# Conv-attention feeding an FFN: a new opening order, gated weight loads, throwaway matmuls and integer sums moved between engines

## Chip, cores and metric

One core of one Trainium2 chip runs the whole kernel. The metric is device time in microseconds (us), the median of the runs. TensorE (PE) multiplies matrices, VectorE (DVE), ScalarE (ACT) and GpSimd (POOL) do elementwise work, SyncE (SP) issues nearly all DMAs.

## Reference

```python
def _attn_ref(x, weight_gen):            # x (4, 4096, 192), weight_gen (4, 4096, 8, 7)
    w = softmax(weight_gen over the last axis)
    x_pad = six zero rows, then x
    out[b, s, h, g] = sum over k of w[b, s, h, k] * x_pad[b, s + k, h, g]   # 8 heads of 24 columns
    return out.reshape(B, S, D)

def _moe_ref(x, w_in, w_out):            # w_in (192, 2048), w_out (2048, 192), both float64 in memory
    h = x @ w_in
    return np.maximum(0.01 * h, h) @ w_out
```

Every token first gets a seven-tap convolution whose taps come out of a softmax, then goes through a two-layer network with a leaky ReLU.

## The kernel before

The 16,384 tokens lie 128 to a partition row. Each of 32 **chunks** takes four rows of every partition (512 tokens); two chunks make one **piece**, which is loaded (`load_weights`, `load_rows`) and put through the softmax together. The convolution of a chunk is seven multiplications and six additions of 768 columns (`conv_ops`); its result is transposed, multiplied by `w_in` (`mm1`), passed through the leaky ReLU (`leak`, `leak_out`) and multiplied by `w_out` (`mm2_...`). Each chunk has eight **steps** (`step(q)`), and a step is one `mm1` with two blocks of 128 hidden units and the `mm2` of earlier blocks.

From chunk 1 on every float32 operand is split into an upper and a lower half (F32R), and three products are summed. Chunk 0 multiplies in plain float32, because the halves of the weights aren't there yet. The weights arrive as float64 words, cut into 16 **keys** of 384 columns, eight of `w_in` and eight of `w_out`, in the order of the list `order`. Each is taken through stages: `read_words` (two ACT instructions, L114 and L115), `widen` (two DVE instructions, L123 and L126), an integer sum (`round_up` on POOL, L137, or L132 on DVE when `widen` is called with `add`), then `upper_half` (L155, ACT) and `lower_half` (L159, DVE), which only chunk 1 and later ones need. `read_words` also issues the load of a later key.

Chunk 0's convolution is shared: heads `0` to `G0` of its 32 row-head groups go to DVE, the others to POOL, and chunk 1's convolution is POOL's alone. The maximum, exponential and sum of the first piece are done in two halves of four rows, `FIRST` and `SECOND`. Later chunks come to TensorE not through its own transposes but by `split_h` (ACT, L307), `split_l` (POOL, L311), `squares` (DVE, L320) and `spread_squares` (L330), four groups of four DMAs from SP for each chunk.

The order in which all engines get their work, up to chunk 2, is written out by hand in the string `START`, one letter an item:

```python
    "ASrrgggggdddddagggggdddrwgggdddddobwTpp"   # start of the string before
```

`A`, `S` are the softmax of `FIRST`, `a`, `b` that of `SECOND`; `d` and `g` are one convolution operation of chunk 0 on DVE and POOL, `p` one of chunk 1 and `q` one of chunks 2 and 3 on POOL; `r`, `w`, `W`, `o`, `u`, `l` are the stages of the next key (`W` is `widen` with the sum on DVE; a capital `U` or `L` puts the half on DVE); `T` and `I` are the PE transposes of chunks 0 and 1 (L291), `k` and `K` the loads of the next piece, `M`, `E`, `D` its softmax, `C`, `V`, `y`, `Y`, `X` the way of chunk 2 to TensorE, and `s` is a step. Engines run their own items in this order and wait for each other by semaphores. `tell` puts a wait into SP's stream: what SP issues after it waits for the instruction told of.

The copies out of the transposes are at L296 and L298, chunk 0's second product at L438, those of later chunks at L399, the split of the hidden units at L373 and L374.

Of the kernel before, what the change touches and what calls it, by code (L numbers as in the profile page):

```python
# [8 lines left out]
F32 = mybir.dt.float32  # L9
F32R = mybir.dt.float32r  # L10
U32 = mybir.dt.uint32
AF = mybir.ActivationFunctionType
ALU = mybir.AluOpType
AX = mybir.AxisListType
PSUM = bass.MemoryType.PSUM

P = 128


HP = P // 2  # L20
# [3 lines left out]

C0 = 1

G0 = 24

NV = 12

START = (
    "ASrrgggggdddddagggggdddrwgggdddddobwTpp"
    "srwoppsrrWWoppKksrrWwoppsrrWwopMp"
    "suLrrWwoEppsuLrrWwoDpsuLuLrrWwoqqqsuLuLwoqqIs"
    "uLuLqqqsuLqqqsuLuLqqCVs"
    "uLuLsyYuLqqsuLXXqqsuLXXqqqsqqs"
)


# [1 line left out]
def conv_attention_moe_kernel(  # L41
# [8 lines left out]
    nc = tc.nc  # L50
    B, S, D = x.shape
    H, K = weight_gen.shape[2:]
    G = D // H
# [4 lines left out]
    PAD = K - 1  # L58
    J = 4
    TOK = J * P  # L60
# [3 lines left out]
    NB = D // HP  # L64
    BK = 32
    NK = P // BK
    HK = H * K
# [27 lines left out]
    def load_words(key, eng=nc.sync):  # L95
        q, kind = key
        if kind == IN:
            w = raw.tile([P, NB, P, 2], U32, tag="wi", name="wi_raw", bufs=3)
            for u, r in enumerate(HALVES):
                f = 2 * q + u  # L100
                eng.dma_start(out=w[r], in_=w_in_words[:, :, f * P:(f + 1) * P, :])
        else:
            w = raw.tile([P, 2, D, 2], U32, tag="wo", name="wo_raw")
            eng.dma_start(out=w, in_=w_out_words[:, 2 * q:2 * q + 2, :, :])
        words[key] = w
# [58 lines left out]
    R = 2 * J  # L164
# [6 lines left out]

    xt, wt, mx, sm = {}, {}, {}, {}

    def load_weights(q):
        r0 = piece[q] * R
        wt[q] = win.tile([P, R, HK], F32, tag="wt", name="wt")
        nc.sync.dma_start(out=wt[q], in_=w_rows[:, r0:r0 + R, :])

    def load_rows(q):
        r0 = piece[q] * R  # L180
        xt[q] = xin.tile([P, PAD + R, D], F32, tag="xt", name="xt")
        if r0 > 0:
            parts = ((0, PAD + R),)
            if q == 0:
                parts = ((PAD, PAD + J), (0, PAD), (PAD + J, PAD + R))
            for a, b in parts:
                nc.sync.dma_start(out=xt[q][:, a:b, :], in_=x_rows[:, r0 - PAD + a:r0 - PAD + b, :])
            return
        nc.sync.dma_start(out=xt[q][:, PAD:, :], in_=x_rows[:, 0:R, :])
        nc.gpsimd.memset(xt[q][0:1, 0:PAD, :], 0.0)  # L190
        for a, b in ((16, P), (1, 16)):
            nc.sync.dma_start(
                out=xt[q][a:b, 0:PAD, :], in_=x_rows[a - 1:b - 1, ROWS - PAD:ROWS, :]
            )
        for b in range(1, B):
            nc.gpsimd.memset(xt[q][b * PB:b * PB + 1, 0:PAD, :], 0.0)
# [3 lines left out]
    def grouped(q, s):  # L200
        return wt[q][:, s, :].rearrange("p r (h k) -> p (r h) k", k=K)
# [4 lines left out]
    def softmax_max(q, s=ALL):  # L206
        if q not in mx:
            mx[q] = win.tile([P, R * H, 1], F32, tag="mx", name="mx")
            sm[q] = win.tile([P, R * H, 1], F32, tag="sm", name="sm")
        m = mx[q][:, s.start * H:s.stop * H, :]  # L210
        nc.vector.tensor_reduce(out=m, in_=grouped(q, s), axis=AX.X, op=ALU.max)  # L211

    def softmax_sub(q, eng, s=ALL):
        eng.tensor_tensor(  # L214
# [12 lines left out]
    def softmax_div(q, eng, s=ALL, out=None):  # L227
        eng.tensor_tensor(  # L228
            out=grouped(q, s) if out is None else out, in0=grouped(q, s),
            in1=spread(sm[q], s), op=ALU.mult,  # L230
        )

    att, twice = {}, {}

    def conv_ops(c, eng, tag, g0=0, g1=J * H, tmp=None, w=None):

        if c not in att:
            att[c] = conv.tile([P, J, D], F32, tag="acc", name="acc", bufs=2)
        acc = att[c].rearrange("p r (h g) -> p (r h) g", g=G)[:, g0:g1, :]
        n = g1 - g0  # L240
        q, i0 = c // 2, c % 2 * J
        if w is None:
            w = wt[q].rearrange("p r (h k) -> p (r h) k", k=K)[:, i0 * H:(i0 + J) * H, :]
        for k in reversed(range(K)):
            xv = xt[q][:, i0 + k:i0 + k + J, :].rearrange("p r (h g) -> p (r h) g", g=G)
            wk = w[:, g0:g1, k:k + 1].to_broadcast([P, n, G])
            if k == K - 1:
                out = acc
            else:
                t = conv.tile([P, n * G], F32, tag=tag, name=tag) if tmp is None else tmp  # L250
                out = t[:, 0:n * G].rearrange("p (h g) -> p h g", g=G)
            eng.tensor_tensor(out=out, in0=xv[:, g0:g1, :], in1=wk, op=ALU.mult)  # L252
            yield
            if k < K - 1:
                if k > 0 or c > 1:
                    eng.tensor_tensor(out=acc, in0=acc, in1=out, op=ALU.add)  # L256
                    yield
                    continue
                if c not in twice:
                    twice[c] = xtp.tile([P, J * NB, 2, HP], F32, tag="sq", name="twice")  # L260
                sums = twice[c][:, g0 * G // HP:g1 * G // HP]
                for u in range(2 - c):
                    eng.tensor_tensor(  # L263
                        out=sums[:, :, u, :], op=ALU.add,
                        in0=att[c].rearrange("p r (b d) -> p (r b) d", d=HP)[:, g0 * G // HP:g1 * G // HP, :],
                        in1=t[:, 0:n * G].rearrange("p (b d) -> p b d", d=HP),
                    )
                yield

    def run(ops, n=None):  # L270
        while (n is None or n > 0) and next(ops, ops) is not ops:
            n = None if n is None else n - 1
# [138 lines left out]
    def tell(ins):  # L411

        told = nc.sync.nop().ins
        tc.add_manual_dep(told, ins.name, after, reason="rows to leave")
        return told
# [90 lines left out]
    with tc.manual_schedule():  # L506
        warm = const.tile([P, 1], F32, name="warm")
        nc.vector.memset(warm, 0.0)
        nc.scalar.activation(out=warm, in_=warm, func=AF.Exp)
        load_weights(0)  # L510
        load_rows(0)
        for key in order[0:4]:
            load_words(key)
        make_identity(nc, ident)
        sm_q = {}
        for q in range(2, NPIECE):
            sm_q[2 * q - 3] = q
# [81 lines left out]
        def spare():  # L599
# [3 lines left out]
            return spares[:, turn[0] % 2, 0:NW]  # L603

        w0 = po0[:, 0, 0:J * HK].rearrange("p (h k) -> p h k", k=K)
        conv0 = dict(
            d=conv_ops(0, nc.vector, None, 0, G0, spares.rearrange("p a b -> p (a b)"), w0),
            g=conv_ops(0, nc.gpsimd, "tmp0", G0, J * H),
            p=conv_ops(1, nc.gpsimd, "tmp"),
        )  # L610
        n, spreads = 0, 0
        for what in START.replace(" ", ""):
            if what in stages:
                prepare(what)
            elif what == "A":
                softmax_max(0, FIRST)
                softmax_sub(0, nc.vector, FIRST)
                softmax_exp(0, FIRST)
            elif what == "S":
                softmax_sum(0, FIRST)  # L620
                softmax_div(0, nc.vector, FIRST, w0[:, 0:J * H, :])
                softmax_div(0, nc.gpsimd, slice(J - C0, J))
            elif what == "a":
                softmax_max(0, SECOND)
                softmax_sub(0, nc.gpsimd, SECOND)
                softmax_exp(0, SECOND)
            elif what == "b":
                softmax_sum(0, SECOND)
                softmax_div(0, nc.gpsimd, SECOND)
            elif what in conv0:  # L630
                run(conv0[what], 1)
            elif what in "TI":
                transposes("TI".index(what))
            elif what == "K":
                load_weights(1)
            elif what == "k":
                load_rows(1)
            elif what == "M":
                softmax_max(1)
                softmax_sub(1, nc.gpsimd)  # L640
            elif what == "E":
                softmax_exp(1)
            elif what == "D":
                softmax_sum(1)
                softmax_div(1, nc.gpsimd)
            elif what == "q":
                feed(3, 1)
            elif what == "C":
                split_h(2)
            elif what == "V":  # L650
                split_l(2, nc.gpsimd)
            elif what in "yY":
                squares(2, "yY".index(what))
            elif what == "X":
                spread_squares(2, [spreads])
                spreads += 1
            elif what == "s":
                step(n)
                n += 1
            else:  # L660
                raise ValueError(what)
# [37 lines left out]
```

## Time and profile before

| | us |
|---|---|
| median of 3 runs | 1177.0 (1175.46 to 1177.43) |
| the profiled execution, its own time | 1179.21 |
| its span, first to last instruction | 1177.2 |
| PE busy | 1144.6 (97%) |
| POOL, ACT, DVE busy | 786.1, 645.7, 515.2 |
| mean granted clock of TensorE | 0.996 |

TensorE is busy nearly all the time, so the kernel can lose time in two ways only: TensorE waits, or it runs at its lower clock. Both happen nearly only in the first 120 us. The profiled execution stands 2.2 us above the median.

### The profile page before, as it was taken

To read this page: it belongs to the slowest core of one execution; us is meant where nothing else is said; L and a number is where in the kernel's file an instruction comes from. 1 tells how busy PE (TensorE), PEld (TensorE's weight loads), DVE (VectorE), ACT (ScalarE), POOL (GpSimd) and SP (SyncE) were. 2 spreads that over 40 slices of the span, in tenths; PEclk is the share of its full clock that TensorE was granted. 3 is DMA by queue.
4 is the path that set the end of the run, shared out by engine and by line. 5 is a ranking of instruction groups with operands and counts; after the bars stand their busy time and mean duration, and the time that the engine had idled before them with its cause. 6 is when DMAs were issued, how large, how long until landed. Compare 5 with 4: busy or idle time off the path is not lost.

```text
span 1177.2 us, 30212 instructions
## 1 busy us (share of the span) xinstructions
PE 1144.6 (97%) x12648; PEld 1072.1 (91%) x12648; DVE 515.2 (44%) x823; ACT 645.7 (55%) x1174; POOL 786.1 (67%) x499
## 2 busy tenths in 40 slices
PE   2998999999999999999999999999999999999998
PEld 1677999999999999999999999999999999999998
DVE  5674444434444434444443444434444433443432
ACT  2655555555555555556555555655555564555554
POOL 5787866678766668766668866667866667966300
PEclk9998999999999999999999999999999999999999
DMA  5612231323323142232323223142241324221220
GB/s 148 187 58 55 69 108 48 105 55 82 110 55 107 45 115 64 69 110 55 99 67 102 76 61 104 45 119 55 69 123 49 103 55 110 68 69 49 53 51 14
DMA packets 42950, 93.70 MB, mean 80 GB/s; under 512 B 9664, under 2 KB 25024, under 8 KB 41023
## 3 DMA queue, kind: packets, MB, share of 16 engines
q1 hardware_dynamic: 42670, 91.59, 28.6%
q8 instruction: 99, 1.62, 0.6%
q14 instruction: 37, 0.29, 0.1%
q10 hardware_dynamic: 144, 0.20, 0.0%
HBM read 31.98 MB, written 12.58 MB: 38 GB/s over the span
## 4 chain that ended last, share of the span: by engine, by line
PE 93%; DVE 2%; POOL 2%; DMA 1%; SPq 1%; issue 1%; ACT 1%; DVEq 0%; POOLq 0%; ACTq 0%
PE hp L351 46%; PE po L399 45%; PE po L438 2%; DMA xt<-in_x_dram 1%; SPq L330 1%; POOL acc L256 1%; POOL tmp L252 1%; DVE spares L252 0%; DVE wo L159 0%; DVE acc L256 0%; DVE gl L374 0%; ACT hp L357 0%; DVE wi_l L159 0%; DMA xx<-sq 0%; POOL bits L137 0%
## 5 line engine op out<-in xcount | busy, mean ns | idle before, releaser
L399 PE MATMUL po<-wo,gh 64*128 64x384 f32 x3968 | 632.2, 354 | 1.6 <-ACT gh L373 1.6
L399 PE MATMUL po<-wo,gl 64*128 64x192 f32 x3968 | 608.2, 248 | 0.7 <-DVE gl L374 0.7
L374 DVE TENSOR_TENSOR gl<-hp,gh 128x512 fp32r<-128x512 f32 x496 | 342.4, 691 | 554.9 <-ACT gh L373 554.9
L399 PEld LDWEIGHTS po<-wo,gh 64*128 64x128 f32 x3968 | 565.8, 185 | 8.1 <-ACT gh L373 1.8
L351 PE MATMUL hp<-xx,wi_h 64*128 64x512 f32 x2976 | 560.5, 397 | 3.7 <-DMA xx<-sq 2.4
L399 PEld LDWEIGHTS po<-wo,gl 64*128 64x128 f32 x3968 | 546.2, 188 | 1.7 <-DVE gl L374 1.5
L357 ACT ACTIVATE hp<-hp 128x512 f32<-128x512 f32 x496 | 292.5, 590 | 426.3 <-PE hp L351 399.3
L351 PE MATMUL hp<-xx,wi_l 64*128 64x512 f32 x1488 | 444.9, 393 | 0.0
L351 PEld LDWEIGHTS hp<-xx,wi_h 64*128 64x128 f32 x2976 | 407.9, 185 | 32.5 <-issue 2.4
L256 POOL TENSOR_TENSOR acc<-acc,tmp 128x768 f32<-128x768 f32 (+1 forms) x190 | 345.5, 1818 | 14.4
L373 ACT CAST gh<-hp 128x512 fp32r<-128x512 f32 x496 | 291.3, 587 | 43.9 <-PE po L399 30.1
L252 POOL TENSOR_TENSOR tmp<-xt,wt 128x768 f32<-128x768 f32 (+1 forms) x192 | 291.5, 1518 | 12.2
L351 PEld LDWEIGHTS hp<-xx,wi_l 64*128 64x128 f32 x1488 | 271.4, 185 | 19.9
L311 POOL TENSOR_TENSOR split<-acc,split 128x768 fp32r<-128x768 f32 x30 | 55.5, 1849 | 170.4 <-ACT split L307 170.4
L475 DVE TENSOR_TENSOR ot<-po,ot 128x384 f32<-128x384 f32 x62 | 34.5, 557 | 76.6 <-ACT ot L474 76.1
L214 POOL TENSOR_TENSOR wt<-wt,mx 128x448 f32<-128x448 f32 (+1 forms) x16 | 15.3, 953 | 72.5 <-DVE mx L211 72.4
L320 DVE STREAM_TRANSPOSE sq<-split 128x384 f32<-128x384 f32 x120 | 58.4, 543 | 0.0
L252 POOL TENSOR_TENSOR acc<-xt,wt 128x768 f32<-128x768 f32 (+1 forms) x32 | 48.5, 1516 | 0.2
L228 POOL TENSOR_TENSOR wt<-wt,sm 128x448 f32<-128x448 f32 (+2 forms) x17 | 15.7, 924 | 39.3 <-DVE sm L225 34.4
L474 ACT COPY ot<-po 128x384 f32<-128x384 f32 x62 | 29.7, 479 | 11.7 <-PE po L399 8.9
L307 ACT CAST split<-acc 128x768 fp32r<-128x768 f32 x30 | 25.1, 838 | 6.9 <-POOL acc L256 6.9
L291 PE MATMUL ta<-ident,twice 128*128 128x128 f32 x24 | 4.3, 351 | 21.6 <-DVE twice L263 21.6
(51 smaller groups left out, 235.9 us busy)
## 6 DMA issues: line engine op xcount, KB each, us to landing
xx<-sq SPq DMA_DIRECT2D x480, 96.0 KB, 2.1
xt<-in_x_dram SPq DMA_DIRECT2D x14, 1344.0 KB, 5.8
out_dram<-ot SPq DMA_DIRECT2D x63, 192.0 KB, 1.9
wt<-in_weight_gen_dram SPq DMA_DIRECT2D x16, 224.0 KB, 2.6
wi_raw<-in_moe_w_in_dram SPq DMA_DIRECT2D x16, 192.0 KB, 8.6
wo_raw<-in_moe_w_out_dram SPq DMA_DIRECT2D x8, 384.0 KB, 4.6
xt<-in_x_dram SPq DMA_DIRECT2D x2, 384.0 KB, 6.7
xt<-in_x_dram SPq DMA_DIRECT2D x1, 768.0 KB, 4.8
```

What stands on the lines that cost most here:

```text
L252: eng.tensor_tensor(out=out, in0=xv[:, g0:g1, :], in1=wk, op=ALU.mult)
L256: eng.tensor_tensor(out=acc, in0=acc, in1=out, op=ALU.add)
L307: nc.scalar.copy(out=split[c][:, 0], in_=att[c])
L311: eng.tensor_tensor(out=l, in0=att.pop(c), in1=h.bitcast(F32), op=ALU.subtract)
L320: nc.vector.transpose(out=sq[c][:, v, i], in_=src[:, v])
L351: nc.tensor.matmul(out=hp[2 * q + u], lhsT=w[s], rhs=r[s], start=(m == 0), stop=(m == len(passes) - 1),)
L357: return nc.scalar.activation(out=hp[n], in_=hp[n], func=AF.Prelu, alpha=0.01).ins
L373: nc.scalar.copy(out=h, in_=t)
L374: nc.vector.tensor_tensor(out=l, in0=t, in1=h.bitcast(F32), op=ALU.subtract)
L399: ins = nc.tensor.matmul(out=po[j // HALF][:, j % HALF, 0:d], lhsT=g[n][s, j * P:(j + 1) * P], rhs=wo[s, f, 0:d], start=(f == 0 and i < HA ...
L474: nc.scalar.copy(out=ot, in_=po[k][:, :, D:2 * D])
L475: nc.vector.tensor_tensor(out=ot, in0=po[k][:, :, 0:D], in1=ot, op=ALU.add)
```

## The change

Six edits, all of them in the opening:

1. The first load takes four rows of the softmax weights and two of the three parts of `x`; the other loads are issued behind a `tell` on the first maximum, and the second half of the softmax weights and the third part of `x` go between the words of `w_in`.
2. Chunk 0's convolution is cut at 20 of 32 groups rather than 24 for taps 6 to 1, and at 24 for tap 0.
3. Twelve products of zeros (`heat`) stand ahead of the transposes of chunk 0, behind the latest DVE operation of its convolution.
4. `W` stands in place of `w` and `o` for 14 of the 16 keys (7 before).
5. Two lower halves go to POOL (`l`), one upper half to DVE (`U`).
6. `START` is reordered: the convolution of chunk 1 is issued in one row, `k` comes ahead of `K`, and `X` stands behind steps 12 and 13 rather than 13 and 14.

```diff
-G0 = 24
+G0 = 20
 START = (
-    "ASrrgggggdddddagggggdddrwgggdddddobwTpp"
-    "srwoppsrrWWoppKksrrWwoppsrrWwopMp"
...
-    "uLuLsyYuLqqsuLXXqqsuLXXqqqsqqs"
+    "ASdrrggggdgddggdggadgdrwgZdgddddgdobTWrppppppppWpkKWrrspWrr..."
...
+    "YLusXqqqXqqsqqXqlXqsqs"
 )
...
-    def load_weights(q):
+    def load_weights(q, s=slice(0, R)):
...
-    def load_rows(q):
+    def load_rows(q, parts=((0, PAD + R),)):
...
-        nc.vector.tensor_reduce(out=m, in_=grouped(q, s), axis=AX.X, op=ALU.max)
+        return nc.vector.tensor_reduce(out=m, in_=grouped(q, s), axis=AX.X, op=ALU.max).ins
...
-    def conv_ops(c, eng, tag, g0=0, g1=J * H, tmp=None, w=None):
+    def conv_ops(c, eng, tag, inner=ALL_G, outer=ALL_G, tmp=None, w=None):
...
         for k in reversed(range(K)):
+            s = inner if k else outer
+            n = s.stop - s.start
...
+            if eng is nc.vector:
+                latest[c] = ins
...
-        load_weights(0)
-        load_rows(0)
-        for key in order[0:4]:
-            load_words(key)
+        load_weights(0, FIRST)
+        load_rows(0, ((PAD, PAD + J), (0, PAD)))
         make_identity(nc, ident)
+        zeros = const.tile([P, TOK], F32R, name="zeros")
+        nc.gpsimd.memset(zeros.bitcast(F32), 0.0)
...
-            d=conv_ops(0, nc.vector, None, 0, G0, spares.rearrange("p a b -> p (a b)"), w0),
-            g=conv_ops(0, nc.gpsimd, "tmp0", G0, J * H),
+            d=conv_ops(0, nc.vector, None, slice(0, G0), slice(0, (J - C0) * H), away, w0),
+            g=conv_ops(0, nc.gpsimd, "tmp", slice(G0, J * H), slice((J - C0) * H, J * H)),
...
+        def heat(n):
+            t = ps_h.tile([P, TOK], F32, tag="h", name="heat")
+            for m in range(n):
+                ins = nc.tensor.matmul(
+                    out=t, lhsT=zeros[:, 0:P], rhs=zeros, start=True, stop=True
+                ).ins
+                if m == 0:
+                    tc.add_manual_dep(ins, latest[0].name, after, reason="not before")
...
             elif what == "A":
-                softmax_max(0, FIRST)
+                tell(softmax_max(0, FIRST))
+                load_words(order[0])
+                load_weights(0, SECOND)
+                load_words(order[1])
+                load_rows(0, ((PAD + J, PAD + R),))
+                load_words(order[2])
+                load_words(order[3])
...
-                softmax_div(0, nc.gpsimd, slice(J - C0, J))
+                softmax_div(0, nc.gpsimd, slice(G0 // H, J))
...
+            elif what == "Z":
+                heat(12)
```

SP's first loads, before and now. `wt` are the softmax weights, `xt` rows of `x`, `wi_raw` and `wo_raw` words of `w_in` and `w_out`; the three `xt` of 768, 1152 and 768 columns are called the first, second and third part.

```order
L177 DMA wt<-in_weight_gen_dram 128x448
L187 DMA xt<-in_x_dram 128x768
L187 DMA xt<-in_x_dram 128x1152
L187 DMA xt<-in_x_dram 128x768
L101 DMA wi_raw<-in_moe_w_in_dram 64x3x256 x6
L104 DMA wo_raw<-in_moe_w_out_dram 128x2x384
```

```order
L176 DMA wt<-in_weight_gen_dram 128x224
L184 DMA xt<-in_x_dram 128x768
L184 DMA xt<-in_x_dram 128x1152
L99 DMA wi_raw<-in_moe_w_in_dram 64x3x256 x2
L176 DMA wt<-in_weight_gen_dram 128x224
L99 DMA wi_raw<-in_moe_w_in_dram 64x3x256 x2
L184 DMA xt<-in_x_dram 128x768
L99 DMA wi_raw<-in_moe_w_in_dram 64x3x256 x2
L102 DMA wo_raw<-in_moe_w_out_dram 128x2x384
```

The first `wt` is half as long, and SP's wait for the first maximum (not shown as a row) stands ahead of the first `wi_raw`.

POOL behind the convolution of chunk 0, before and now. `acc<-xt,wt` and `tmp<-xt,wt` are multiplications of chunk 1's convolution, `acc<-acc,tmp` its additions, `bits<-bits,rnd` the integer sums of keys.

```order
L228 TENSOR_TENSOR wt<-wt,sm 128x224
L252 TENSOR_TENSOR acc<-xt,wt 128x768
L252 TENSOR_TENSOR tmp<-xt,wt 128x768
L137 TENSOR_TENSOR bits<-bits,rnd 128x384
L256 TENSOR_TENSOR acc<-acc,tmp 128x768
L252 TENSOR_TENSOR tmp<-xt,wt 128x768
L137 TENSOR_TENSOR bits<-bits,rnd 128x384
L256 TENSOR_TENSOR acc<-acc,tmp 128x768
```

```order
L225 TENSOR_TENSOR wt<-wt,sm 128x224
L251 TENSOR_TENSOR acc<-xt,wt 128x768
L251 TENSOR_TENSOR tmp<-xt,wt 128x768
L256 TENSOR_TENSOR acc<-acc,tmp 128x768
L251 TENSOR_TENSOR tmp<-xt,wt 128x768
L256 TENSOR_TENSOR acc<-acc,tmp 128x768
```

Before, an integer sum stood between the operations of the convolution, and POOL waited there for DVE; now the convolution runs without one.

DVE behind the copy out of chunk 0's transposes (`xx<-ta`), before and now. `spares<-mag` and the row after it are `widen`, `bits<-spares,rnd` is the integer sum.

```order
L296 COPY xx<-ta 128x4x128
L123 TENSOR_SCALAR spares<-mag 128x384
L126 SCALAR_TENSOR_TENSOR bits<-mag,spares 128x384
L123 TENSOR_SCALAR spares<-mag 128x384
L126 SCALAR_TENSOR_TENSOR spares<-mag,spares 128x384
L132 ISA bits<-spares,rnd 128x768
```

```order
L295 COPY xx<-ta 128x4x128
L121 TENSOR_SCALAR spares<-mag 128x384
L124 SCALAR_TENSOR_TENSOR spares<-mag,spares 128x384
L130 ISA bits<-spares,rnd 128x768
L121 TENSOR_SCALAR spares<-mag 128x384
L124 SCALAR_TENSOR_TENSOR spares<-mag,spares 128x384
L130 ISA bits<-spares,rnd 128x768
```

Each key now has three DVE instructions here; nine keys in a row are made so, with one maximum between them.

## Rows read from the trace of the kernel before

**Rows 1.** Who PE waited for, from 0 to 140 us.
```profile
PE ta L291 <- DVE twice L263: 21.6, 1, 21.6
PE hp L351 <- DMA xx<-sq: 2.4, 2, 1.9
PE po L399 <- ACT gh L373: 1.6, 1, 1.6
PE hp L351 <- DVE xx L301: 1.4, 1, 1.4
PE hp L351 <- POOL bits L137: 0.6, 1, 0.6
PE po L399 <- DVE gl L374: 0.6, 2, 0.3
```
**Rows 2.** Windows of PE: stretch, its length, busy (instructions), granted clock, DMA share, GB/s.
```profile
95.08:98.50 3.42, 3.42 (x20) 0.50 0.02 5
112.16:119.00 6.84, 6.33 (x33) 0.50 0.08 19
...
119.00:1170.00 1051.00, 1050.84 (x11981) 1.00 0.28 76
```
**Rows 3.** Timeline of PE: start, duration, instruction, count, idle time before it.
```profile
21.65 2.79 PE L291 MATMUL ta<-ident,twice 128*128 128x128 f32 x12 [21.65 <-DVE twice L263]
24.37 6.62 PE L351 MATMUL hp<-xx,bits 64*128 64x512 f32 x24
31.58 2.85 PE L351 MATMUL hp<-xx,bits 64*128 64x512 f32 x12 [0.59 <-POOL bits L137]
34.36 2.87 PE L438 MATMUL po<-bits,g 128*128 128x192 f32 x16
```
**Rows 4.** Timeline of PE at the seam to chunk 1, and the window of one `mm1`.
```profile
65.01 1.53 PE L291 MATMUL ta<-ident,twice 128*128 128x128 f32 x12
...
76.01:78.21 2.20, 2.20 (x20) 1.00 0.31 110
```
**Rows 5.** DMA issues from 1.2 to 2.0 us: size and us to landing.
```profile
xt<-in_x_dram SPq DMA_DIRECT2D x1, 576.0 KB, 8.6
```
**Rows 6.** Windows of the DMAs: stretch, its length, granted clock, DMA share, GB/s.
```profile
2.00:5.50 3.50, 1.00 0.91 307
```
**Rows 7.** Timelines of DVE and POOL in chunk 0's convolution.
```profile
3.41 0.39 DVE L211 TENSOR_REDUCE mx<-wt 128x32 f32<-128x224 f32 x1 [2.54 <-DMA wt<-in_weight_gen_dram]
6.25 0.28 POOL L228 TENSOR_TENSOR wt<-wt,sm 128x56 f32<-128x56 f32 x1 [4.93 <-DVE po L228]
10.26 0.76 DVE L252 TENSOR_TENSOR spares<-xt,po 128x576 f32<-128x576 f32 x1 [3.37 <-DMA xt<-in_x_dram]
20.08 1.42 DVE L263 TENSOR_TENSOR twice<-acc,spares 128x576 f32<-128x576 f32 x2
```
**Rows 8.** Operations of POOL by form, from 0 to 92 us: busy, mean ns, idle before.
```profile
L256 POOL TENSOR_TENSOR acc<-acc,tmp 128x768 f32<-128x768 f32 x11 | 20.6, 1874 | 0.4
L252 POOL TENSOR_TENSOR tmp<-xt,wt 128x768 f32<-128x768 f32 x12 | 19.4, 1618 | 0.6
L137 POOL TENSOR_TENSOR bits<-bits,rnd 128x384 uint32<-128x384 uint32 x9 | 9.0, 999 | 9.0 <-DVE bits L126 9.0
L256 POOL TENSOR_TENSOR acc<-acc,tmp 128x192 f32<-128x192 f32 x5 | 2.9, 590 | 0.4
```
**Rows 9.** DVE from 22 to 67.58 us: the window, then its integer sums.
```profile
22.00:67.58 45.58, 30.31 (x50) 1.00 0.51 149
...
L132 DVE CUSTOM_DVE_ANT_0 bits<-spares,rnd 128x768 uint16<-128x768 uint16 x7 | 3.9, 557 | 0.3
```
**Rows 10.** Timeline of POOL: the last addition of chunk 2's convolution.
```profile
89.22 1.84 POOL L256 TENSOR_TENSOR acc<-acc,tmp 128x768 f32<-128x768 f32 x1
```
**Rows 11.** Timeline of SP, and the chain of waits: chunk 2's way to TensorE.
```profile
101.68 10.13 SPq L330 DMA_DIRECT2D xx<-sq  x16
...
111.22 2.12 DMA xx<-sq
```

More of the change, by code (lines that the diff above doesn't have):

```diff
@@ L25 @@
 C0 = 1
-G0 = 24
+G0 = 20
 NV = 12
 START = (
-    "ASrrgggggdddddagggggdddrwgggdddddobwTpp"
-    "srwoppsrrWWoppKksrrWwoppsrrWwopMp"
-    "suLrrWwoEppsuLrrWwoDpsuLuLrrWwoqqqsuLuLwoqqIs"
-    "uLuLqqqsuLqqqsuLuLqqCVs"
-    "uLuLsyYuLqqsuLXXqqsuLXXqqqsqqs"
+    "ASdrrggggdgddggdggadgdrwgZdgddddgdobTWrppppppppWpkKWrspWrrWsrrsWWMrpspWr"
+    "WruspLrUuWrLWuEsDrwrLsouWWuLLuqqWlqquqsqLLqquqqqIusLLusuqsLuLquCVyuqqLsL"
+    "YLusXqqqXqqsqqXqlXqsqs"
 )
@@ L172, in conv_attention_moe_kernel @@
     xt, wt, mx, sm = {}, {}, {}, {}
-    def load_weights(q):
+    def load_weights(q, s=slice(0, R)):
         r0 = piece[q] * R
-        wt[q] = win.tile([P, R, HK], F32, tag="wt", name="wt")
-        nc.sync.dma_start(out=wt[q], in_=w_rows[:, r0:r0 + R, :])
-    def load_rows(q):
+        if q not in wt:
+            wt[q] = win.tile([P, R, HK], F32, tag="wt", name="wt")
+        nc.sync.dma_start(out=wt[q][:, s, :], in_=w_rows[:, r0 + s.start:r0 + s.stop, :])
+    def load_rows(q, parts=((0, PAD + R),)):
         r0 = piece[q] * R
-        xt[q] = xin.tile([P, PAD + R, D], F32, tag="xt", name="xt")
+        if q not in xt:
+            xt[q] = xin.tile([P, PAD + R, D], F32, tag="xt", name="xt")
         if r0 > 0:
-            parts = ((0, PAD + R),)
-            if q == 0:
-                parts = ((PAD, PAD + J), (0, PAD), (PAD + J, PAD + R))
             for a, b in parts:
@@ L231, in softmax_div @@
         )
-    att, twice = {}, {}
-    def conv_ops(c, eng, tag, g0=0, g1=J * H, tmp=None, w=None):
+    att, twice, latest = {}, {}, {}
+    ALL_G = slice(0, J * H)
+    def conv_ops(c, eng, tag, inner=ALL_G, outer=ALL_G, tmp=None, w=None):
         if c not in att:
             att[c] = conv.tile([P, J, D], F32, tag="acc", name="acc", bufs=2)
-        acc = att[c].rearrange("p r (h g) -> p (r h) g", g=G)[:, g0:g1, :]
-        n = g1 - g0
+        acc = att[c].rearrange("p r (h g) -> p (r h) g", g=G)
         q, i0 = c // 2, c % 2 * J
@@ L244, in conv_ops @@
         for k in reversed(range(K)):
+            s = inner if k else outer
+            n = s.stop - s.start
             xv = xt[q][:, i0 + k:i0 + k + J, :].rearrange("p r (h g) -> p (r h) g", g=G)
-            wk = w[:, g0:g1, k:k + 1].to_broadcast([P, n, G])
+            wk = w[:, s, k:k + 1].to_broadcast([P, n, G])
             if k == K - 1:
-                out = acc
+                out = acc[:, s, :]
             else:
-                t = conv.tile([P, n * G], F32, tag=tag, name=tag) if tmp is None else tmp
+                t = conv.tile([P, J * D], F32, tag=tag, name=tag) if tmp is None else tmp
                 out = t[:, 0:n * G].rearrange("p (h g) -> p h g", g=G)
-            eng.tensor_tensor(out=out, in0=xv[:, g0:g1, :], in1=wk, op=ALU.mult)
+            ins = eng.tensor_tensor(out=out, in0=xv[:, s, :], in1=wk, op=ALU.mult).ins
+            if eng is nc.vector:
+                latest[c] = ins
             yield
[L254 to L267, printed above, removed]
-                yield
+            if k > 0 and k < K - 1 or k == 0 and c > 1:
+                eng.tensor_tensor(out=acc[:, s, :], in0=acc[:, s, :], in1=out, op=ALU.add)
+                yield
+        if c > 1:
+            return
+        if c not in twice:
+            twice[c] = xtp.tile([P, J * NB, 2, HP], F32, tag="sq", name="twice")
+        b = slice(outer.start * G // HP, outer.stop * G // HP)
+        av = att[c].rearrange("p r (b d) -> p (r b) d", d=HP)[:, b, :]
+        ov = t[:, 0:n * G].rearrange("p (b d) -> p b d", d=HP)
+        for u in range(2 - c):
+            eng.tensor_tensor(out=twice[c][:, b, u, :], in0=av, in1=ov, op=ALU.add)
+        yield
     def run(ops, n=None):
@@ L605, in conv_attention_moe_kernel @@
         w0 = po0[:, 0, 0:J * HK].rearrange("p (h k) -> p h k", k=K)
+        away = spares.rearrange("p a b -> p (a b)")
         conv0 = dict(
-            d=conv_ops(0, nc.vector, None, 0, G0, spares.rearrange("p a b -> p (a b)"), w0),
-            g=conv_ops(0, nc.gpsimd, "tmp0", G0, J * H),
+            d=conv_ops(0, nc.vector, None, slice(0, G0), slice(0, (J - C0) * H), away, w0),
+            g=conv_ops(0, nc.gpsimd, "tmp", slice(G0, J * H), slice((J - C0) * H, J * H)),
             p=conv_ops(1, nc.gpsimd, "tmp"),
         )
+        def heat(n):
[6 more added lines that the diff above has]
+                    tc.add_manual_dep(ins, latest[0].name, after, reason="not before")
         n, spreads = 0, 0
```

## Prediction, made before the changed kernel had run

> **What bounds the kernel now.** I read three views in this order. First, who PE waited for, from 0 to 140 us: 21.6 us for the first convolution, 0.6 for an integer sum on POOL, 1.4 for DVE's subtraction behind chunk 1's transposes, 1.6 and 0.6 for split hidden units, 2.4 for the DMAs that bring chunk 2 [rows 1]. Second, the windows: from 119 to 1170 us PE is busy 1050.84 of 1051.00 us at the full clock, so nothing can be gained there, while in two earlier stretches of 3.42 and 6.84 us the granted clock is 0.50 (1.2 of 2.4 GHz); both come behind waits of PE [rows 2]. Third, PE's own timeline: twelve transposes take 2.79 us at 21.65 but 1.53 in chunk 1, and the first 24 records of L351 take 6.62 us where twelve take 2.85 later [rows 3, 4]. The window view shows no lower level there, but these durations are those of the lower one. So the time is the start of the first transposes, plus PE's work, plus what is lost before 119 us. An edit counts only if it moves PE.
>
> **Part by part.**
>
> *Gated loads.* The second part of `x` lands 8.6 us after its issue [rows 5]; DVE waits 3.37 us for it, until 10.26 [rows 7]. Up to that part 224 + 384 + 576 = 1184 KB were issued; at 307 GB/s from 2.0 us they are through near 6.0 [rows 6], yet it landed at 10.2, with words moving beside it. Now 1072 KB go alone, through near 5.5 at the same rate. The bounds of the landing are thus 5.5 and 9.9 (10.24 less 112 KB at 307 GB/s). Anything up to 6.8 costs nothing, because DVE is in its first multiplication until then; I take that. What the wait on SP holds back are the words: they are issued behind the maximum, which ends at 3.80 [rows 7]; the first needed is widened behind DVE's fourth tap, at 11.3 by the next parts. So they may take some 6 us to land before the gate costs anything.
>
> The Trainium skill, page "DMA: Bandwidth & Descriptors", section "Queues, rings and completion order", says that each DMA engine consumes a queue's descriptors in ring order. By that rule what is issued behind the second part could not delay it, and the gate would bring only the 112 KB. The 4.2 us between 6.0 and 10.2 speak against it, though one late engine would look the same.
>
> *The convolution of chunk 0.* On DVE it lasted from 10.26 to 21.50 (the end of its last row) [rows 7], 11.24 us; ten of its operations shrink from 576 to 480 columns, by about 0.10 us each (0.76 us at 576, 0.39 for a reduction of 224), so 10.2 us remain: 6.8 + 10.2 = 17.0. POOL gets 288 columns instead of 192. An addition is 0.59 us at 192 and 1.87 at 768, so 0.80 at 288; a multiplication is 1.62 against 1.87, so 0.70 [rows 8]. With 0.08 between instructions five pairs are 8.3; the division (0.4, from 0.28 at 56), the first multiplication (0.7), the subtraction (0.6), tap 0 (0.6) and the doubled sum (1.1) make it 11.7 us from POOL's start at 6.25: 17.9. POOL ends last, and the transposes start at 17.9 instead of 21.65: **-3.8**. If the rows land at 9.9, DVE ends last at 20.1, and the term is -1.5.
>
> *Throwaway products.* They wait for DVE's fourth tap: 6.8 + four operations of 0.69 + the maximum 0.3 + two of 0.69 = 11.3. Eighteen products of half height, two side by side, take 2.2 us [rows 4], so one of 512 columns is 0.24 us at the full clock and 0.49 at the lower: twelve last 2.9 to 5.9 and end between 14.2 and 17.2. They hold up nothing; a gap of 0.7 to 3.7 us follows. If the clock is up when the transposes run, the gain is 2.79 - 1.53 = 1.3 there and 6.62 - 2 x 2.79 = 1.0 in the first products [rows 3, 4]: 2.3. If it isn't, 0. A loss is excluded, since PE ran there at the lower clock before. If it rises and falls again in the gap, one more stretch like that of 3.42 us [rows 2] takes 1.7 of the 2.3 back. I take the middle, **-1.2**, because both stretches at 0.50 came behind waits of about 2 us [rows 1], which is the middle of the gap.
>
> *Integer sums.* Seven of POOL's nine go; the nine were 9.0 us of work and 9.0 of waiting for DVE [rows 8]. PE's wait of 0.6 for one ends, since DVE makes the third key 5.3 us behind the transposes' start (the copy at 1.7, six instructions of 0.6) and PE wants it after 1.5 + 2 x 2.79 = 7.1: **-0.6**. DVE pays 7 x 0.56 = 3.9 us, a lower half more (about 1) and an upper half (0.6) on 30.3 us busy of 45.6 [rows 9], with some 3 us between its instructions: about 39. PE's chunk 0 is 1.5 + 14 x 2.79 = 40.5 us of work [rows 3], so DVE has 41. It fits, narrowly, if the words come in time. The 1.4 us at chunk 1's transposes came about because DVE still had a key to widen; I let 0.4 stand: **-1.0**, with bounds of -1.4 and +4.
>
> *The way to chunk 2.* POOL ended chunk 2's convolution at 91.06 [rows 10], and ACT, whose split of it stands ahead of two blocks of hidden units, kept PE waiting from about 91.5. With 16 us less of sums and waiting, some 1 us for a lower half taken over and up to 4 of waiting for the next piece's softmax, POOL ends between 75 and 80. PE is 6.6 us earlier by then and wants those blocks near 84.9. So the waits of 1.6 and 0.6 go, and with them the 3.42 us at half clock (1.7): **-3.9**. SP's sixteen DMAs were issued from 101.68 and landed 11.7 us later [rows 11], while PE had two steps of work from the products they are told of to chunk 2. A step is 4.4 us (239 of them in the 1051 us of [rows 2]): 8.8 us. The DMAs now stand one step earlier, so 13.2 us of work cover 11.7. The 2.4 us go, and with them 6.84 us at half clock with 6.33 busy (3.2): **-5.6**; as the margin is only 1.5 us, the other bound is 0.
>
> *The order of `k` and `K`, the upper half on DVE and the cut at 24 for tap 0* lie inside these sums.
>
> Sum: -3.8 - 1.2 - 0.6 - 1.0 - 3.9 - 5.6 = -16.1. Against the profiled execution's own 1179.2 that is 1163.1; it stands 2.2 above the median, so I forecast **1161** us.
>
> **Rivals.** (A) *The rows land no earlier* (ring order, as above, or a late engine): the first term is -1.5, the time 1163.3. For it: 8.6 us is long even for shared engines. (B) *The spread still ends last ahead of chunk 2*, because SP's DMAs need DVE's four transposes of squares, which stand behind more work: 1161 + 5.6 = 1166.6. (C) *DVE is late at chunk 1's transposes*: the wait of 1.4 stays or grows to 4, and a fall of the clock adds 1.7: up to 1167.7. (D) *Slower: DVE sets the pace of chunk 0.* PE wants a key every 2.79 us. A key costs DVE 1.8, and from the eighth on a lower half besides. Should a lower half cost over 1.0 on the mean beside POOL, PE waits in each product, its clock falls, and chunk 0's last ten products of 2.79 take 28 us more: 1161 + 28 = 1189. Against it: 39 us of work in 41. (E) *The savings don't reach PE*: what is gained ahead is waited for at a later chain that doesn't move; 1177. Against it: from 119 us on nothing but PE is full [rows 2].
>
> **Chances.** Forecast 0.45, A 0.17, B 0.15, C 0.13, D 0.06, E 0.04. What a measurement of this kernel can tell from no change is about 0.2%, 2.4 us. The forecast, A, B and C lie below that: faster 0.90; E is the same, 0.04; D is slower, 0.06. The range: with the throwaway products at their best (1.1 more), the remaining 0.4 gone and 1 to 2 us for an earlier start of POOL behind the smaller first load and the spread of the runs, the low end is 1156; B or C with the products bringing nothing ends at 1170. D and E are left out.
>
> **What would show it.** Right: DVE's second multiplication starts near 6.8 us; the transposes start near 18 and take under 2 us; PE's waits for POOL and for the DMAs of squares are gone; no stretch at 0.50 between 70 and 120 us; chunk 2 starts near 98 us instead of 113. Wrong: a second multiplication at 9 us or later (A); PE waiting for the DMAs of squares (B), or long for the subtraction behind chunk 1's transposes (C); PE waiting for integer sums on DVE throughout chunk 0 (D).

## The result, and the profile after

The changed kernel takes **1159.87 us** in the median of 4 runs (1159.32 to 1161.17), beside 1176.23 of four runs of the kernel before: a ratio of 0.9869, 95% interval [0.9842, 0.9897]. The forecast was 1161 us, with a range of 1156 to 1170. The profiled execution is the longest of the four, 1161.17 us, with a span of 1159.4.

Page of the changed kernel, part 1: busy time, share and instructions of each engine.

```profile
PE 1142.1 (99%) x12660; PEld 1023.7 (88%) x12660; DVE 514.2 (44%) x829; ACT 645.1 (56%) x1173; POOL 782.2 (67%) x495
```

Who PE waited for, from 0 to 130 us (in total, times, longest), all that is listed:

```profile
PE heat L614 <- DVE spares L251: 10.6, 1, 10.6
PE ta L290 <- DVE twice L266: 2.1, 1, 2.1
```

Of the six waits of [rows 1] only the first is left, cut in two by the throwaway products. From the transposes on PE waits for nothing. Timeline of PE (start, duration, count, idle time before):

```profile
10.56 4.52 PE L614 MATMUL heat<-zeros 128*128 128x512 f32 x12 [10.56 <-DVE spares L251]
17.19 2.80 PE L290 MATMUL ta<-ident,twice 128*128 128x128 f32 x12 [2.10 <-DVE twice L266]
19.91 8.35 PE L350 MATMUL hp<-xx,bits 64*128 64x512 f32 x36
28.19 2.87 PE L437 MATMUL po<-bits,g 128*128 128x192 f32 x16
...
58.76 1.47 PE L290 MATMUL ta<-ident,twice 128*128 128x128 f32 x12
...
68.44 0.73 PE L350 MATMUL hp<-xx,wi_h 64*128 64x512 f32 x4
...
98.08 0.65 PE L350 MATMUL hp<-xx,wi_h 64*128 64x512 f32 x4
```

These starts, set beside those of [rows 2 to 4], split the difference of the spans, 1177.2 - 1159.4 = 17.8 us:

| stretch | before | after | difference | forecast |
|---|---|---|---|---|
| start to chunk 0's transposes | 21.65 | 17.19 | -4.46 | -3.8 |
| to the first product of `mm2` | 12.71 | 11.00 | -1.71 | -1.2 and -0.6 |
| to chunk 1's transposes | 30.65 | 30.57 | -0.08 | 0 |
| to chunk 1's second `mm1` | 11.00 | 9.68 | -1.32 | -1.0 |
| to chunk 2's first full `mm1`, and to the end | 37.43 + 1063.76 | 29.64 + 1061.32 | -10.23 | -3.9 and -5.6 |

Part of this belongs to the execution of the kernel before that was profiled, which has two stretches at half clock, of 3.42 and 6.84 us [rows 2]. A second profiled execution of that kernel (experiment 8) has one of 3.4 us and a span of 1174.3; against it the last row is -7.82 and the whole difference 14.9.

Windows of PE, columns as in [rows 2]:

```profile
13.84:17.26 3.42, 1.32 (x7) 1.00 1.12 255
17.26:20.67 3.41, 3.41 (x14) 0.50 0.26 53
...
68.44:98.08 29.64, 29.64 (x335) 1.00 0.27 68
...
108.00:1152.00 1044.00, 1043.71 (x11906) 1.00 0.28 77
```

One stretch at half clock is left, and it falls on the transposes: the throwaway products brought the clock up at 13.84 and it fell again at 17.26. Both later stretches of [rows 2] are gone; from 68.44 to 98.08 PE has no idle time at all.

What the first term rested on: the landing of the second part of `x` (column as in [rows 5]), then the timelines of DVE and POOL.

```profile
xt<-in_x_dram SPq DMA_DIRECT2D x1, 576.0 KB, 5.1
```
```profile
6.82 0.66 DVE L251 TENSOR_TENSOR spares<-xt,po 128x480 f32<-128x480 f32 x1 [0.55 <-DMA xt<-in_x_dram]
15.71 1.42 DVE L266 TENSOR_TENSOR twice<-acc,spares 128x576 f32<-128x576 f32 x2
...
5.74 0.38 POOL L225 TENSOR_TENSOR wt<-wt,sm 128x112 f32<-128x112 f32 x1 [3.96 <-DVE po L225]
16.10 1.14 POOL L266 TENSOR_TENSOR twice<-acc,tmp 128x192 f32<-128x192 f32 x2
```

The part lands in 5.1 us instead of 8.6, DVE's second multiplication starts at 6.82 instead of 10.26 [rows 7], and both engines end the convolution within 0.11 us (17.13 and 17.24).

What the other terms rested on: the window of chunk 0 (busy time of PE, PEld, DVE, ACT, POOL), and DVE's groups by form in it (busy, mean ns, idle before).

```profile
17.20:58.76 41.56, 41.56 (x204) 26.87 (x205) 36.98 (x60) 26.17 (x54) 35.70 (x25) 0.96 0.55 169
```
```profile
L130 DVE CUSTOM_DVE_ANT_0 bits<-spares,rnd 128x768 uint16<-128x768 uint16 x14 | 7.8, 557 | 0.8
L157 DVE TENSOR_TENSOR wi_l<-bits,wi_h 128x384 fp32r<-128x384 f32 x5 | 5.2, 1048 | 0.6 <-ACT wi_h L153 0.6
L157 DVE TENSOR_TENSOR wo<-bits,wo 128x384 fp32r<-128x384 f32 x2 | 2.5, 1266 | 0.0
```

Then the seam to chunk 1 and the way of chunk 2, on the timelines of DVE, POOL and SP:

```profile
60.02 1.89 DVE L300 TENSOR_TENSOR xx<-ta,xx 128x512 fp32r<-128x512 f32 x3 [2.34 <-ACT xx L299]
...
74.02 1.84 POOL L256 TENSOR_TENSOR acc<-acc,tmp 128x768 f32<-128x768 f32 x1
...
85.27 10.12 SPq L329 DMA_DIRECT2D xx<-sq  x16
```

DVE is done early enough to stand idle for 2.34 us at the seam. POOL ends chunk 2's convolution at 75.86, where [rows 10] has 91.06, and SP's sixteen DMAs are issued from 85.27 to 95.39, before PE wants chunk 2 at 98.08.

### The profile page after: what moved, and what is told of

The parts are those of the page before. It is cut to its first block, busy times and chain, and to the rows that moved or that the text cites. A ratio compares the mean times of both kernels' runs of the same rounds, so it can differ in the third digit from the quotient of the medians.

```text
span 1159.4 us, 30227 instructions
## 1 busy us (share of the span) xinstructions
PE 1142.1 (99%) x12660; PEld 1023.7 (88%) x12660; DVE 514.2 (44%) x829; ACT 645.1 (56%) x1173; POOL 782.2 (67%) x495
## 4 chain that ended last, share of the span: by engine, by line
PE 98%; DVE 1%; DMA 0%; ACT 0%; issue 0%; SPq 0%; DVEq 0%
PE po L398 48%; PE hp L350 47%; PE po L437 2%; DMA xt<-in_x_dram 0%; DVE spares L251 0%; DVE acc L256 0%; PE ta L290 0%; DVE twice L266 0%; ACT hp L356 0%; DVE gl L373 0%; DVE xx L300 0%; ACT gh L372 0%; ACT xx L299 0%; DVE ot L474 0%; DVE bits L124 0%
## 5 line engine op out<-in xcount | busy, mean ns | idle before, releaser
L398 PE MATMUL po<-wo,gh 64*128 64x384 f32 x3968 | 581.3, 353 | 0.0
L398 PE MATMUL po<-wo,gl 64*128 64x192 f32 x3968 | 497.8, 248 | 0.3 <-DVE gl L373 0.3
L350 PE MATMUL hp<-xx,wi_h 64*128 64x512 f32 x2976 | 472.8, 395 | 0.1
L398 PEld LDWEIGHTS po<-wo,gl 64*128 64x128 f32 x3968 | 378.4, 187 | 11.1 <-DVE gl L373 0.5
L398 PEld LDWEIGHTS po<-wo,gh 64*128 64x128 f32 x3968 | 372.7, 184 | 11.8
L350 PEld LDWEIGHTS hp<-xx,wi_h 64*128 64x128 f32 x2976 | 260.2, 184 | 46.3 <-DVE xx L300 0.4
L350 PE MATMUL hp<-xx,wi_l 64*128 64x512 f32 x1488 | 294.3, 391 | 0.0
L350 PEld LDWEIGHTS hp<-xx,wi_l 64*128 64x128 f32 x1488 | 140.1, 184 | 33.0
L437 PEld LDWEIGHTS po<-bits,g 128*128 128x128 f32 x128 | 20.6, 190 | 4.9 <-DVE spares L121 1.5
```

The costliest lines, as they stand in the source:

```text
L350: nc.tensor.matmul(out=hp[2 * q + u], lhsT=w[s], rhs=r[s], start=(m == 0), stop=(m == len(passes) - 1),)
L398: ins = nc.tensor.matmul(out=po[j // HALF][:, j % HALF, 0:d], lhsT=g[n][s, j * P:(j + 1) * P], rhs=wo[s, f, 0:d], start=(f == 0 and i < HA ...
L437: nc.tensor.matmul(out=po0[:, j // 2, j % 2 * D:(j % 2 + 1) * D], lhsT=g_h[n][:, j * P:(j + 1) * P], rhs=value((n // 2, OUT))[:, n % 2], s ...
```

## The experiments

Each edit was made either to the changed kernel ("after") or to the kernel before. Ratios are against runs of the kernel before on the same chip.

**1. After, without the gate.**

```diff
-                tell(softmax_max(0, FIRST))
+                softmax_max(0, FIRST)
```

> The changed kernel without SP's wait for the first maximum; the loads keep their new order. Theory (what is issued behind delays the rows of x): the second part lands at 8.5 to 10 us instead of 6.8, DVE's second multiplication starts then, and the transposes start near 19 instead of 17.2; the time rises by 1 to 3 us. Rival (ring order: what is issued behind can't delay it): the second part still lands by 7.1 us, the transposes start at 17.2 to 17.5, and the time is within 0.5 us.

Measured: 1160.66 us (1160.13 to 1161.74), ratio 0.9871 [0.9854, 0.9887]. Timelines of DVE and PE:

```profile
7.56 0.66 DVE L251 TENSOR_TENSOR spares<-xt,po 128x480 f32<-128x480 f32 x1 [1.26 <-DMA xt<-in_x_dram]
...
17.92 2.82 PE L290 MATMUL ta<-ident,twice 128*128 128x128 f32 x12 [2.30 <-DVE twice L266]
```

Without any wait on SP the rows are there 0.74 us later, and the time is 0.8 us above that of after. So the gate was not what brought the rows from 10.26 to 6.82; what remained was the halved first load, which experiments 7 and 8 try. Neither expectation was met: the transposes start at 17.92, between the 17.5 of the one and the 19 of the other.

**2. After, without the throwaway products.**

```diff
-    "ASdrrggggdgddggdggadgdrwgZdgddddgdobTW..."
+    "ASdrrggggdgddggdggadgdrwgdgddddgdobTW..."
```

> The changed kernel without the twelve throwaway products. Theory (they raised the clock, and it fell again in the gap of 2.1 us): the transposes start at 17.2 as before and still take 2.8 us, the first 36 records of L350 take 8.9 to 9.6 us instead of 8.35, and the time rises by 0.5 to 1.2 us. Rival (they gained nothing at all): 8.35 us and no difference. In both no wait appears elsewhere.

Measured: 1162.24 us (1161.62 to 1163.18), ratio 0.9886 [0.9872, 0.9901], 2.4 us above after. Timeline of PE:

```profile
16.98 2.79 PE L290 MATMUL ta<-ident,twice 128*128 128x128 f32 x12 [16.98 <-DVE twice L266]
19.70 8.43 PE L350 MATMUL hp<-xx,bits 64*128 64x512 f32 x36
28.07 2.87 PE L437 MATMUL po<-bits,g 128*128 128x192 f32 x16
```

The transposes take 2.79 us, as the theory said, but the 36 products take 8.43, near the rival's 8.35, and the time rises by more than either gave. From the transposes to the first product of `mm2` this execution takes 11.09 us, after's 11.00: in the two profiled executions the twelve products gained 0.1 us there.

**3 and 4. After, with sixteen and with twenty throwaway products** (`heat(12)` becomes `heat(16)`, `heat(20)`).

> Sixteen throwaway products instead of twelve, so that they end near 16 us when the clock rises early, and near 17.4 when it doesn't; the gap ahead of the transposes is 0 to 1.2 us. Theory (the gap made the clock fall): it stays up, the transposes take 1.5 us and the first 36 records of L350 8.35 or less, and the time falls by 1.0 to 1.8 us. Rival (transposes themselves, or the moment at which the record begins, decide): they take 2.8 us as with twelve, and the time doesn't change.

> Twenty throwaway products. Theory: no gap is left; the transposes take 1.5 us. If the clock rises late the products last until near 19 us and put the transposes off by up to 2 us, so the time falls by 0 to 1.8 us, less evenly than with sixteen. Rival (as for sixteen): transposes of 2.8 us, and a time that is the same or up to 2 us longer.

Measured: 1159.47 us (1159.22 to 1160.28), ratio 0.9863 [0.9849, 0.9878], and 1159.63 us (1159.31 to 1160.17), ratio 0.9864 [0.9849, 0.9879]. Timelines of PE with sixteen, then with twenty:

```profile
10.57 5.64 PE L614 MATMUL heat<-zeros 128*128 128x512 f32 x16 [10.57 <-DVE spares L251]
17.19 1.53 PE L290 MATMUL ta<-ident,twice 128*128 128x128 f32 x12 [0.98 <-DVE twice L266]
18.65 8.00 PE L350 MATMUL hp<-xx,bits 64*128 64x512 f32 x36
```
```profile
9.87 6.82 PE L614 MATMUL heat<-zeros 128*128 128x512 f32 x20 [9.87 <-DVE spares L251]
16.89 1.58 PE L290 MATMUL ta<-ident,twice 128*128 128x128 f32 x12 [0.19 <-DVE twice L266]
```

With sixteen the clock stays up: against after's profiled execution the transposes take 1.27 us less and the 36 products 0.35 less, and the span is 1157.8, 1.6 shorter. The medians differ by only 0.4 us. The other three of after's four runs have spans of 1157.5 to 1158.6, below the 1159.8 to 1161.4 of the four runs without products, which fits a clock that stayed up in them; they have no trace that would show it, and their mean granted clock, 0.999 to 1.000, doesn't tell, as the runs without products have the same. Sixteen products gave the lowest median of all kernels, but by less than the runs scatter. That the products are worth something is shown on one chip: sixteen are 2.8 us faster than none, and every run with them is faster than every run without.

**5. After, with the `X` moved back toward the end.**

```diff
-    "YLusXqqqXqqsqqXqlXqsqs"
+    "YLusqqqqqsXXqqqlqsXXqs"
```

> The changed kernel with the sixteen DMAs of chunk 2 one step later, behind steps 13 and 14 as before the change. Theory (a chain of 11.7 us against 8.8 us of work): PE waits 2.4 to 3 us for the DMAs of squares ahead of chunk 2, the clock falls behind it for 3.4 to 6.8 us, and the time rises by 4 to 6 us. Rival (the earlier end of the convolution alone removed the wait): no wait of PE, the time within 1 us.

Measured: 1165.72 us (1165.57 to 1166.64), ratio 0.9914 [0.9894, 0.9935], 5.85 us above after. Who PE waited for:

```profile
PE hp L350 <- DMA xx<-sq: 4.2, 2, 3.3
```

The wait of [rows 1] for the DMAs of squares is back, larger than before, and a stretch of 3.4 us at half clock behind it (it costs half of that, 1.7): 4.2 + 1.7 = 5.9. The place of `X` alone carries the term that the prediction put at 5.6; the parts differ, as the prediction had 2.4 of waiting and 3.2 of lost clock, so that the sums agree this closely is partly luck.

**6. After, with seven integer sums back on POOL**, each right behind its `W` in the order written out:

```diff
-    stages["W"] = lambda key: widen(key, True)
+    BACK = [order[i] for i in (1, 2, 6, 8, 10, 14, 15)]
+    def widen_whole(key):
+        widen(key, key not in BACK)
+        if key in BACK:
+            round_up(key)
+    stages["W"] = widen_whole
```

> The changed kernel with the integer sums of the seven keys that had them on POOL before put back there, at the same places of the order. Theory (POOL waits for DVE between operations of the convolution): PE waits for sums on POOL in chunk 0, chunk 2's convolution on POOL ends 7 to 16 us later than the 75.9 of the changed kernel, ACT's split of it holds the hidden units up, and the time rises by 2 to 8 us. Rival (the new order of the convolutions did it, not the engine of the sums): POOL ends by 84 us, no wait of PE for ACT or POOL beyond 0.6 us, the time within 1.5 us.

Measured: 1174.33 us (1173.38 to 1175.08), ratio 0.998 [0.997, 0.999]: 14.5 us above after, far more than either theory gave. Who PE waited for, and the timelines of DVE and POOL:

```profile
PE hp L350 <- POOL bits L135: 11.6, 1, 11.6
```
```profile
20.88 0.55 DVE L124 SCALAR_TENSOR_TENSOR bits<-mag,spares 128x384 uint32<-128x384 uint32 x1
...
21.21 1.54 POOL L251 TENSOR_TENSOR acc<-xt,wt 128x768 f32<-128x768 f32 x1
...
33.23 1.54 POOL L251 TENSOR_TENSOR tmp<-xt,wt 128x768 f32<-128x768 f32 x1
34.73 0.99 POOL L135 TENSOR_TENSOR bits<-bits,rnd 128x384 uint32<-128x384 uint32 x1
```

DVE has the third key widened at 21.43, but its sum on POOL comes at 34.73: the eight operations of chunk 1's convolution, issued in one row, stand ahead of it. With the sums in these places PE waits 11.6 us behind the long row. An order with the sums on POOL between the operations of that row was not tried.

**7. Before, with the new loads and the gate alone**: the halved first load, the `tell` and the new order of SP's loads, as in the diff of the change.

> The kernel before with the gated loads alone, everything else as before. Theory (each part of the opening moves PE by itself): DVE's second multiplication starts near 6.8 us, the transposes start near 18.1 instead of 21.65, PE's later waits keep their size, and the time falls by 3 to 3.6 us. Rival (what is gained ahead is waited for at a chain that doesn't move): the transposes start early, but PE waits longer at chunk 1's seam or at chunk 2, which still starts near 113 us, and the time falls by less than 1 us.

Measured: 1173.73 us (1171.09 to 1175.18), ratio 0.9979 [0.9968, 0.999]: 2.6 us, a little less than the theory's 3 to 3.6; PE's later waits keep their size (2.8 for squares, 1.6 for ACT, 1.4 at the seam). DVE's second multiplication and the transposes start 2.46 and 2.47 us earlier than in [rows 3, 7]:

```profile
7.80 0.76 DVE L251 TENSOR_TENSOR spares<-xt,po 128x576 f32<-128x576 f32 x1 [1.44 <-DMA xt<-in_x_dram]
...
19.18 2.79 PE L290 MATMUL ta<-ident,twice 128*128 128x128 f32 x12 [19.18 <-DVE twice L262]
```

**8. Before, with the halved first load alone**, no gate, the words behind all rows as before; and the kernel before once more beside it (one run of each).

```diff
-        load_weights(0)
+        load_weights(0, FIRST)
         load_rows(0)
+        load_weights(0, SECOND)
         for key in order[0:4]:
```

> The kernel before with the first load of softmax weights cut in half, the other half behind the third part of x, and no gate. Theory (the 112 KB ahead count at the rate of 307 GB/s, and the rest is chance): the maximum starts near 2.9 us instead of 3.4, and the second part lands 0.4 us earlier than in the kernel before, within the chance that the other look shows. Rival (the smaller load is what mattered): the second part lands by 7 us and the transposes start by 18.5 us.

> The kernel before once more, for its first 25 us. Theory (one late DMA engine, another amount each time): the second part of x lands somewhere between 7.5 and 10.3 us, other than 10.24 by over 0.5 us, and the transposes move with it. Rival (what is queued behind it, always the same): DVE's second multiplication starts at 10.0 to 10.5 us again.

Measured: 1172.37 us in the one, which is below all nineteen runs of the kernel before on that chip (1173.22 to 1178.83), and 1176.34 in the other. The rows with the halved load: landing, DVE, PE and PE's later waits; last, PE in the kernel before once more.

```profile
xt<-in_x_dram SPq DMA_DIRECT2D x1, 576.0 KB, 4.4
```
```profile
6.27 0.76 DVE L253 TENSOR_TENSOR spares<-xt,po 128x576 f32<-128x576 f32 x1
...
17.64 2.79 PE L292 MATMUL ta<-ident,twice 128*128 128x128 f32 x12 [17.64 <-DVE twice L264]
```
```profile
PE hp L352 <- DMA xx<-sq: 2.8, 2, 2.0
PE po L400 <- ACT gh L374: 1.6, 1, 1.6
```
```profile
23.88 5.72 PE L351 MATMUL hp<-xx,bits 64*128 64x512 f32 x24
...
75.55 0.73 PE L351 MATMUL hp<-xx,wi_h 64*128 64x512 f32 x4
```

With no gate at all DVE no longer waits for the part. Over all profiled executions it landed in 6.8 to 8.6 us where the first load was whole (four executions of three kernels) and in 4.4 to 6.1 where it was halved (nine). With the halved load it took 4.4 and 5.9 without a gate (experiments 8 and 1) and 4.4 to 6.1 with one. So it was the halved load, the rival of the first expectation; for the gate nothing beyond this scatter was seen. In the kernel before once more the multiplication started at 9.78, between its two expectations. The later waits keep their size when the start moves by 4 us, so a start gained is not given back: the span, 1170.6, is 3.7 us shorter than that of the kernel before once more, whose transposes start at 21.16, 3.5 us later.

**9. Before, with all integer sums but the first on DVE** (every `w` becomes `W`, every `o` after the first is dropped; the order otherwise the same).

> The kernel before with all integer sums but the first on DVE and the order otherwise as it was. Theory (POOL's waits for DVE were what made chunk 2 late): PE's wait of 0.6 us for POOL goes, POOL ends chunk 2's convolution 8 to 16 us earlier than 91.06, PE's waits of 1.6 and 0.6 us for hidden units go with the stretch at half clock behind them, the wait of 2.4 us for the DMAs of squares stays, and the time falls by 3.5 to 5 us. Rival (the new order did it): POOL ends by at most 4 us earlier, PE still waits for ACT's split, the time falls by under 1.5 us. Third possibility: DVE gets late, PE waits for it at chunk 1's seam for over 2 us.

Measured: 1176.12 us (1173.34 to 1178.02), ratio 1.0002 [0.9989, 1.0016]: nothing. Who PE waited for, then who POOL waited for:

```profile
PE hp L350 <- DMA xx<-sq: 2.8, 2, 2.1
PE hp L350 <- DVE xx L300: 2.7, 1, 2.7
```
```profile
POOL wt L213 <- DVE mx L210: 13.3, 3, 6.0
POOL wt L227 <- ACT wi_h L154: 7.8, 1, 7.8
```

PE's waits for POOL (0.6) and for ACT (1.6) are gone, but that for DVE at chunk 1's seam grew from 1.4 to 2.7, and POOL, freed of its sums, waits longer for the softmax of the next pieces instead (its wait for the maximum was 5.3 before) and ends chunk 2's convolution at 89.65, not at 75 to 80.

**10. The same, with `X` also moved ahead** (behind steps 12 and 13).

```diff
-    "rrWWqqqsuLuLWqqIsuLuLqqqsuLqqqsuLuLqqCVsuLuLsy"
-    "YuLqqsuLXXqqsuLXXqqqsqqs"
+    "rrWWqqqsuLuLWqqIsuLuLqqqsuLqqqsuLuLqqCVsuLuLyY"
+    "sXXuLqqsuLXXqqsuLqqqsqqs"
```

> The run before this one, and the sixteen DMAs of chunk 2 behind steps 12 and 13, with its squares ahead of step 12. Theory (both terms add): no wait of PE for ACT or for the DMAs of squares, no stretch at half clock between 70 and 120 us, and the time falls by 8 to 10.5 us against the kernel before; the opening keeps its start near 21 us. Rival (squares stand in DVE's way): PE still waits over 1 us for the DMAs of squares or for split hidden units, and the time falls by under 6 us.

Measured: 1176.05 us (1173.15 to 1178.34), ratio 1.0007 [0.9994, 1.002]. PE's wait for the DMAs of squares is gone; what it waited for instead:

```profile
PE po L398 <- SPq L412: 2.8, 3, 1.6
PE hp L350 <- DVE xx L300: 2.7, 1, 2.7
PE po L398 <- DVE gl L373: 1.6, 3, 1.1
```

The seam is as late as in experiment 9, with 6.8 us at half clock from 66.55 on, and DVE is late for the split of hidden units. The longest of these waits in total is a new one, for SP: PE's products wait for a `tell` (L412) in SP's stream, and two of the three waits (0.79 and 0.43 us) fall while SP issues the DMAs of squares, from 98.96 to 109.10, the third (1.60, at 133.07) while it issues those of the next chunk. The moved sums and the moved `X` were thus both there without the new order of the rest, and nothing came of them.

## Why the prediction was right, point by point

- **Bound.** Right: PE is full at the full clock from 20.67 us to 1155, and what moved PE came through to the end. Rival E falls with that, and experiment 8 shows it by itself.
- **Gated loads, -3.8.** The size held (-4.46), and 6.8 for the landing was met at 6.82, but that is luck: the reason failed. It was "what the wait on SP holds back are the words", whose traffic had been taken as the cause of the late landing. The halved first load did it (experiments 1 and 8), and the step that reckoned those 112 KB at 307 GB/s, some 0.4 us, is the one that was wrong; they are worth 2 to 3 us. The rule of ring order, which the prediction took from the Trainium skill, page "DMA: Bandwidth & Descriptors", section "Queues, rings and completion order", fits the gate, for which no gain beyond the scatter was seen. Rival A's price for an unmoved landing came from the same 0.4 us and was wrong with it. Of the 4.46 us 3.44 are the landing and 1.02 the shorter convolution, which takes 10.37 us from the second multiplication to the transposes, where it took 11.39 and, with the loads alone, 11.38 (experiment 7). The remaining -0.7 against the forecast is POOL: forecast to end at 17.9, it started at 5.74 rather than 6.25 and ended at 17.24.
- **Throwaway products, -1.2.** In the profiled execution the case came that the prediction described, the clock up and down again in the gap: the transposes are at 2.80, so the sign that they take under 2 us failed there. The stretch behind them is 1.71 us shorter, of which 0.59 is POOL's wait, but the other 1.1 can't be put down to the products: without any the stretch is nearly as short (11.09, experiment 2), and the first 24 products took 6.62 us in one execution of the kernel before and 5.72 in another. By the medians the products are worth 2.4 (experiment 2; 2.0 by the ratios, whose intervals overlap), and sixteen of them 2.8: the prediction's best case of 2.3, not its middle.
- **Integer sums, -0.6 and -1.0.** The sizes held (the 0.59 wait is gone; -1.32 at the seam, where 0.4 had been left standing). That the moved sums end POOL's wait is shown by experiment 9; the seam they make worse by themselves (2.7 instead of 1.4 there), so its gain needs the new order too. Rival D is refuted: DVE's 36.98 us of work fit in 41.56, against 39 in 41. The seven lower halves took 1.11 us on the mean, over the 1.0 at which D had PE wait, and PE didn't wait.
- **The way to chunk 2, -3.9 and -5.6.** The two together were sized well: -10.23 against -9.5, or -7.82 by the other execution of the kernel before (the forecast took 2.2 us off its whole sum for that); POOL ends at 75.86 (forecast 75 to 80) and chunk 2 starts at 98.08 (forecast 98). That the place of `X` is worth 5.6 is shown (5.85, experiment 5). The step "with 16 us less of sums and waiting" is wrong as a cause by itself: with the sums gone and the order kept, POOL ends 1.4 us earlier instead of 11 to 16 (experiment 9). What differs is the new order, which brings the words, the maximum and the convolution of chunk 1 forward as well; which of these POOL needs is not shown. That order, as written, in turn needs the sums on DVE (experiment 6). The prediction let only the order of `k` and `K` "lie inside these sums" and gave the rest of the new order no term; it was a condition of both.
- **Rivals B and C.** Neither came. B's price is that of experiment 5 (forecast 1166.6, measured 1165.72), though there `X` was moved by hand; B's cause, squares that come late on DVE, was not tried. C is real in the old order: the 2.7 us at the seam of experiments 9 and 10.

Left open: which part of the new order lets DVE be on time at chunk 1's seam, and why 112 KB less at the front hasten a later load by 2 to 3 us. For the first, no order between the two was tried; for the second, no other size of the first load.

## What to carry to other kernels

Taking work off an engine that others wait for paid here only together with an order behind it that uses the room: the moved sums alone brought nothing, the whole change with seven of them left on POOL 2 us, although its transposes start 4.8 us earlier, and the whole change 16. Before crediting a freed engine with an earlier end, look up what it waits for next. And load ahead only what the first instructions need: here the second half of a load that was not wanted yet delayed a part that was.

## What the runs showed of the hardware

- A load of 576 KB landed 6.8 to 8.6 us after its issue behind a first load of 224 KB, and 4.4 to 6.1 behind one of 112 KB; 112 KB are 0.4 us at the 307 GB/s of [rows 6].
- Products of zeros raised the clock that is granted: the transposes took 1.53 us behind sixteen of them and 2.79 behind none (experiments 3 and 2). With twelve it fell again about when the transposes began where PE had been idle for 2.1 and 2.3 us (after, experiment 1), and stayed up where the idle time was 1.3 and 1.7 us (experiments 5 and 6) or, with more products, 1.0 and 0.2 us (experiments 3 and 4).
- The subtraction of a lower half on DVE, 128x384, took 1.05 us on the mean for `w_in` and 1.27 for `w_out` in chunk 0, with POOL at work for 35.70 of chunk 0's 41.56 us, while the integer sums held 0.56.
